# Batch 1's score products in a block-sparse attention and MLP kernel: four 64x64 array tiles, or the whole array with zeros in q

## The chip, the cores and the metric

The kernel runs on one core of one Trainium2 chip. The metric is the device time of one launch in microseconds. The notes below use the engines' short names: TensorE (PE in the profile, PEld its weight loads), VectorE (DVE), ScalarE (ACT), GpSimd (POOL), and SyncE (SP), which issues most of the DMAs.

## The reference

Three stages follow one another. The attention has 2 batches, 8 heads, 768 positions and a head size of 64. Each query sees the keys within 16 positions of its own, and 24 block keys (the maximum over each block of 32 keys), whose values are block means:

```python
k_sum = k.reshape(B, H, nb, block, D).max(axis=3)
v_sum = v.reshape(B, H, nb, block, D).mean(axis=3)
scores_l = scale * np.matmul(q, k.transpose(0, 1, 3, 2))
mask_l = np.abs(pos[:, None] - pos[None, :]) < window
scores_s = scale * np.einsum('bhsd,bhnd->bhsn', q, k_sum) + np.log(block)
...
out = softmax(concat([where(mask_l, scores_l, -1e9), scores_s])) @ concat([v, v_sum])
```

The result, as 2 x 768 rows of 512, goes through a gated two-layer network (token shift with mu, w_k of 512x1024, a squared relu, w_v, and a sigmoid gate by w_r) and then through a mixer (w_tok1, w_tok2 over positions, w_ch1 and w_ch2 over channels, 512x1536 and back). All is f32.

## The kernel before

**Attention.** Work goes by tiles of 128 queries: 6 tiles for each batch. Heads are taken in pairs: the 128 partitions of q and k hold the 64 values of head 2p on rows 0 to 63 and those of head 2p+1 on rows 64 to 127, for four pairs p. A tile of 128 queries needs two key ranges, one for each half of 64 queries: 96 local keys and 24 block keys, 120 columns in all (NC). `kw` holds keys and block keys so that the range of half 0 starts at column 0 and that of half 1 at WC - NC; `k_max` (VectorE) and `kw_sums` (POOL, L293) write the block keys.

`s_stage` (L355 to L391) makes the scores. Before, each product takes the 64 rows of one head and 64 queries and writes 64 partitions of a PSUM bank, so it uses a quarter of TensorE's array; the four combinations of head and half use the four quarters. In batch 0 the stage runs for one head of each pair at a time (`es` has one member), in batch 1 for both heads at once, with 16 matmuls per tile and their order on the queue fixed by `in_line`. There are two score banks (tag "s"), one for each head e. After the products VectorE adds the mask, scales and finds the minimum (L385, four per bank), ScalarE takes the exponential and the row sums (L387), POOL normalizes in batch 1 (`n_stage`, L399), TensorE transposes (`t_stage`, L405), and `v_stage` (L425) multiplies with the values into the bank "pv", which ScalarE copies to `xT`.

**Order.** `attention()` and `main()` are generators. `main()` makes the first network: `ko` matmuls (hidden layer, in groups of 24), `k2_tile` (squared relu) and `values` (`acc` matmuls, in groups of 12). The loop at L674 takes steps of `main()` by a credit after each step of `attention()`, and a weight step (`weights.step`, with ScalarE, VectorE and POOL work) now and then. The final order on each engine is made by a planner that simulates the program with its own costs; `after` and `behind` are ordering hints to it. An engine's queue is in order. SP's queue issues the loads: `q_load` (L353), `k_load`, `vt_load`, `vw_load`. `prep_next` places batch 1's first loads during batch 0; later query tiles are loaded two tiles ahead, into three buffers (QB).

**Masks.** Three masks (inner, first and last tile) are made at L645 to L663 on POOL; rows 0 to 63 hold half 0 and rows 64 to 127 half 1.

Of the kernel before, what the change touches and what calls it, by code (L numbers as in the profile page):

```python
# [9 lines left out]
F32 = mybir.dt.float32  # L10
# [4 lines left out]
ALU = mybir.AluOpType  # L15
# [39 lines left out]


@with_exitstack
def fused_kernel(ctx, tc, q, k, v, vt, mu, w_k, w_v, w_r, w_t1, w_t2, w_c1, w_c2, out):
    nc = tc.nc
    B, NT = q.shape[:2]  # L60
    S, DM = v.shape[1] - WINDOW * 2, v.shape[2]
    H, D = 8, 64
    DFF = w_v.shape[0]
# [158 lines left out]
    def in_line(inst):  # L222

        behind(inst, line[-1:])
        line.append(inst)
# [7 lines left out]
    def after(inst):  # L233

        behind(inst, mark[-1:])
# [31 lines left out]
    def st_of(b):  # L267
        if b not in state:
            state[b] = {"kw": {}, "qT": {}, "vw": {}, "pv": {}, "den": {}}
            state[b]["ks"] = at.tile([128, NP, NB], F32, tag="ks", bufs=2, name="ks")  # L270
        return state[b]
# [17 lines left out]
    @ahead(HK)  # L289
    def kw_sums(b, t):  # L290
        st = state[b]
        for o in (0, WC - NB):
            nc.gpsimd.tensor_scalar(st["kw"][t][:, :, o:o + NB], st["ks"], 1.0, 1.0, ALU.mult, ALU.mult)  # L293
# [53 lines left out]
    @ahead(HL)  # L347
    def q_load(b, t):
        if b == 0:
            st_of(b)["qT"][t] = xT[:, :, XB + 1 + 128 * t:XB + 129 + 128 * t]  # L350
        else:
            st_of(b)["qT"][t] = at.tile([128, NP, 128], F32, tag="qT", bufs=QB, name="qT")
        after(nc.sync.dma_start(st_of(b)["qT"][t], q[b, t]))  # L353

    @ahead(HS)  # L355
    def s_stage(b, t, es):
        st = state[b]
        mask = masks[1 if t == 0 else 2 if t == NT - 1 else 0]
        kw, qT = st["kw"][t], st["qT"][t]
        sps = [bank("s", 2, [128, NP, NC], "sp") for _ in es]  # L360
        line.clear()
        for p in range(NP):
            for half in range(2):
                c0 = half * (WC - NC)
                for sp, e in zip(sps[::-1], es[::-1]):
                    r = slice(64 * e, 64 * e + 64)
                    m = nc.tensor.matmul(sp[64 * half:64 * half + 64, p], qT[r, p, 64 * half:64 * half + 64],  # L367
                                         kw[r, p, c0:c0 + NC], start=True, stop=True)
                    if len(es) > 1:
                        in_line(m)  # L370
        if PINL:
            mark.append(m)
        zs = []
        for sp, e in zip(sps, es):
            mn = at.tile([128, NP], F32, tag="mn", bufs=4, name="mn")
            if b not in LATE:
                den = at.tile([128, NP], F32, tag="den", bufs=4, name="den")
            else:
                if e == 0:
                    st["den"][t] = at.tile([128, 2, NP], F32, tag="dens", bufs=3, name="dens")  # L380
                den = st["den"][t][:, e]
            P = []
            for p in range(NP):
                pe = at.tile([128, NC], F32, tag="pe", bufs=PEB, name="pe")
                low = nc.vector.tensor_tensor_reduce(out=pe, in0=sp[:, p], in1=mask, op0=ALU.add, op1=ALU.min,  # L385
                                                     scale=-1.0 / math.sqrt(D), scalar=3.0e38, accum_out=mn[:, p:p + 1])
                nc.scalar.activation(pe, pe, AF.Exp, bias=mn[:, p:p + 1], scale=-1.0, accum_out=den[:, p:p + 1])  # L387
                P.append(pe)
            lows.append(low)
            zs.append({"u": (b, t, e), "P": P, "den": den})  # L390
        return zs  # L391
# [20 lines left out]
    @ahead(HV)  # L412
    def v_stage(zs):
        b, t, _ = zs[0]["u"]
        st = state[b]
        if t not in st["pv"]:
            st["pv"][t] = bank("pv", 1, [128, NP, 128], "pv")
        pv = st["pv"][t]
        line.clear()
        for p in range(NP):  # L420
            for half in range(2):
                for z in zs[::-1]:
                    e = z["u"][2]
                    h = 2 * p + e
                    m = nc.tensor.matmul(pv[64 * e:64 * e + 64, p, 64 * half:64 * half + 64],  # L425
                                         st["vw"][t][half][0][:, h * D:(h + 1) * D],
                                         z["PT"][:, p, 64 * half:64 * half + 64], start=True, stop=True)
                    if len(zs) > 1:
                        in_line(m)
        if zs[-1]["u"][2] == 1:  # L430
            c0 = b * XB + 1 + 128 * t
            if b not in LATE:
                nc.scalar.copy(xT[:, :, c0:c0 + 128], pv)
            else:
                den = st["den"].pop(t)
                nc.vector.tensor_scalar(den, den, 1e-9, None, ALU.add)
                nc.vector.reciprocal(den, den)
                rb = bank("pt", 2, [128, NP, 128], "rb")
                for p in range(NP):
                    for e in range(2):  # L440
                        nc.tensor.matmul(rb[64 * e:64 * e + 64, p], den[:, e, p:p + 1].to_broadcast([128, D]), ident,
                                         start=True, stop=True)
                x = xT[:, :, c0:c0 + 128]
                nc.scalar.copy(x, pv)
                nc.vector.tensor_tensor(x, x, rb, ALU.mult)
# [64 lines left out]
            q_load(b, 1)  # L510

    def prep(b):

        for t in range(NT):
            k_max(b, t)
            yield HOLD / (NT + 2)
        for j in range(2):
            vt_sum(b, j)
            yield HOLD / (NT + 2)
        kw_sums(b, 0)  # L520
        v_gather(b)
# [120 lines left out]
            q_load(0, t + 1)  # L642
    while weights.todo:
        weights.load()
    masks = []  # L645
    for kind in range(3):
        mc = at.tile([128, NC], F32, name=f"mask{kind}")
        mm = work.tile([128, 2, 128], F32, tag="t32", bufs=2, name="mm")
        for half in range(2):
            m = mm[:, half, :NC]  # L650
            nc.gpsimd.memset(m, 0.0)
            first = 64 * half - PAD
            keys = m[:, NB:NC] if half == 0 else m[:, 0:NK]
            for base, cm, st in ((first + EDGE, -1, 1), (EDGE - first, 1, -1)):
                nc.gpsimd.affine_select(out=keys, in_=keys, pattern=[[st, NK]], compare_op=ALU.is_ge, fill=-8.0 * BIG,
                                        base=base, channel_multiplier=cm)
            if kind == 1 and half == 0:
                nc.gpsimd.memset(m[:, NB:NB + PAD], -8.0 * BIG)
            if kind == 2 and half == 1:
                nc.gpsimd.memset(m[:, NK - PAD:NK], -8.0 * BIG)  # L660
            nc.gpsimd.memset(m[:, 0:NB] if half == 0 else m[:, NK:NC], math.sqrt(D) * math.log(BLOCK))
            nc.gpsimd.tensor_scalar(mc[64 * half:64 * half + 64], m[64 * half:64 * half + 64], 1.0, 1.0, ALU.mult, ALU.mult)
        masks.append(mc)  # L663
    for t in range(NT):
        ahead(HK)(k_max)(0, t)
    kw_sums(0, 0)
    for z in range(B):
        nc.gpsimd.memset(xT[:, :, z * XB:z * XB + 1], 0.0)
    nc.gpsimd.tensor_scalar(oms, mus, -1.0, 1.0, ALU.mult, ALU.add)
# [412 lines left out]
    for got in cd():  # L1082
# [10 lines left out]
    const.release()  # L1093


_INS = ['q', 'k', 'v', 'vt', 'mu', 'moe_w_k', 'moe_w_v', 'moe_w_r',
        'moe2_w_tok1', 'moe2_w_tok2', 'moe2_w_ch1', 'moe2_w_ch2']


def laid_out(q, k, v, mu_k, mu_r, w_k):  # L1100

    import numpy as np

    B, H, S, D = q.shape
    nt = S // 128

    def by_values(x):
        return x.reshape(B, H // 2, 2, x.shape[2], D).transpose(0, 2, 4, 1, 3).reshape(B, 2 * D, H // 2, x.shape[2])

    pad = ((0, 0), (0, 0), (WINDOW, WINDOW), (0, 0))  # L1110
    kp = by_values(np.pad(k, pad))
    dm, dff = w_k.shape
    return {
        "q": by_values(q).reshape(B, 2 * D, H // 2, nt, 128).transpose(0, 3, 1, 2, 4),
        "k": np.stack([kp[..., 128 * t:128 * t + 128 + 2 * WINDOW] for t in range(nt)], axis=1),
        "v": np.pad(v, pad).transpose(0, 2, 1, 3).reshape(B, S + 2 * WINDOW, H * D),
        "vt": by_values(v).reshape(B, 2 * D, 2, H // 4 * S).transpose(0, 2, 1, 3),
        "mu": np.concatenate([m.reshape(-1, 128).T for m in (mu_k, mu_r)], axis=1),
        "moe_w_k": w_k.reshape(dm // 128, 128, dff // 128, 128).transpose(2, 1, 0, 3).reshape(dff // 128, 128, dm),
    }  # L1120
# [22 lines left out]
```

## Time and profile before

| | |
|---|---|
| median of 3 runs | 503.41 us |
| runs | 502.32 to 503.72 us |
| profiled execution, span | 502.8 us |
| profiled execution, own time beside its span | not listed apart from the runs above; the median is 0.6 us over the span |
| mean granted TensorE clock | 0.990 of full speed |
| TensorE, VectorE, ScalarE, POOL busy | 97%, 63%, 50%, 43% |

The span runs from the first to the last instruction of one profiled execution. Matmuls are pipelined and their recorded durations overlap, so what one costs is read from the distance between starts. In the rows, "64*64 64x120" means weights of 64 rows by 64 columns and a moving operand of 64 partitions by 120 columns. A bracket at the end of a row is the idle time ahead of it and what ended it; "issue" means that the profile shows no releaser. f32 matmuls are recorded as two instructions each, transposes as one.

### The profile page before, as it was taken

Reading aid. Unit: us, or ns where it says so; the run is one execution under the profiler, and the core shown is the slowest. Engines: PE = TensorE matmul, PEld = TensorE weight load, DVE = VectorE, ACT = ScalarE, POOL = GpSimd, SP = SyncE. Lnnn points to the kernel's source line nnn. Section 1 sums busy time; section 2 is a strip of 40 time slices with the busy share of each in tenths; the row PEclk is TensorE's granted clock in tenths of the full one; section 3 lists DMA queues with packets and bytes.
Section 4 is the critical chain, followed back from the end, with each engine's and each line's share of the span. In section 5 each row is a group of like instructions: output and inputs, shape, how many; then the busy total and the mean of one; then the engine's idle time right before and its main releaser. Section 6 shows DMA issues by size and latency. Waiting matters only on the chain.

```text
span 502.8 us, 8800 instructions
## 1 busy us (share of the span) xinstructions
PE 487.9 (97%) x3278; PEld 407.1 (81%) x3278; DVE 316.6 (63%) x638; ACT 250.9 (50%) x569; POOL 217.4 (43%) x266
## 2 busy tenths in 40 slices
PE   7999997999999999999999998999999999999996
PEld 3567785888888888888888887878898999989995
DVE  2888998641514355598889789646579638354352
ACT  1778746862544555686585455454554435111110
POOL 6335587862441447345516434774942813000000
PEclk9899998899999999999999999999999999999999
DMA  8999930221000650000551998639351405253102
GB/s 264 323 309 361 335 87 14 88 80 40 20 1 2 224 196 0 1 0 14 161 163 21 400 394 313 211 112 316 117 168 42 142 31 164 52 200 117 52 1 83
DMA packets 35914, 70.63 MB, mean 140 GB/s; under 512 B 3072, under 2 KB 12288, under 8 KB 35872
## 3 DMA queue, kind: packets, MB, share of 16 engines
q1 hardware_dynamic: 34288, 69.09, 42.0%
q10 hardware_dynamic: 1584, 0.98, 0.7%
q8 instruction: 26, 0.43, 0.3%
q14 instruction: 16, 0.13, 0.1%
HBM read 60.04 MB, written 9.44 MB: 138 GB/s over the span
## 4 chain that ended last, share of the span: by engine, by line
PE 75%; DMA 10%; DVE 8%; POOL 2%; ACT 2%; issue 1%; SPq 1%; DVEq 0%; POOLq 0%
PE ko L544 13%; PE acc L544 13%; PE o L955 12%; PE m L544 11%; PE o L983 7%; PE ro L544 7%; PE go L544 5%; DMA wst<-in_moe_w_k_dram 3%; DMA xT<-in_q_dram 3%; DMA ybuf<-in_v_dram 2%; DVE wf L163 2%; PE pv L425 2%; PE sp L367 2%; PE h L544 2%; DMA wst<-in_moe_w_ch_dram 1%
## 5 line engine op out<-in xcount | busy, mean ns | idle before, releaser
L175 POOL TENSOR_TENSOR w<-wf,w 128x512 fp32r<-128x512 f32 x50 | 69.1, 1387 | 77.3 <-ACT w L174 72.4
L544 PE MATMUL ko<-xh,w 128*128 128x256 f32 x384 | 76.3, 288 | 1.7 <-POOL w L175 0.9
L544 PE MATMUL m<-u,w 128*128 128x256 f32 x504 | 65.1, 283 | 0.8 <-DVE mw L846 0.7
L544 PEld LDWEIGHTS m<-u,w 128*128 128x128 f32 x504 | 63.4, 191 | 2.9 <-DVE mw L846 0.9
L544 PEld LDWEIGHTS ko<-xh,w 128*128 128x128 f32 x384 | 61.1, 188 | 5.4 <-POOL w L175 1.1
L544 PE MATMUL acc<-w,kh 128*128 128x512 f32 x192 | 61.7, 404 | 0.0
L955 PE MATMUL o<-w,gh 128*128 128x512 f32 x192 | 59.1, 391 | 0.0
L544 PE MATMUL ko<-xl,w 128*128 128x256 f32 x192 | 54.4, 283 | 1.1 <-DVE xl L536 1.1
L559 POOL TENSOR_TENSOR kl<-rl,kh 128x512 fp32r<-128x512 f32 x24 | 33.7, 1405 | 44.6 <-ACT kh L558 36.4
L163 DVE SCALAR_TENSOR_TENSOR wf<-wst,wf 128x512 int32<-128x512 int32 x50 | 47.6, 956 | 8.2 <-ACT wst L153 7.1
L174 ACT CAST w<-wf 128x512 fp32r<-128x512 f32 x50 | 30.9, 620 | 42.8 <-DVE wf L163 40.9
L557 DVE TENSOR_TENSOR rl<-rl 128x512 f32<-128x512 f32 x24 | 19.6, 819 | 48.4 <-ACT rl L556 48.2
L387 ACT ACTIVATE pe<-pe,mn 128x120 f32<-128x120 f32 x96 | 36.6, 383 | 14.6 <-DVE mn L385 14.3
L153 ACT ACTIVATE wst<-wst 128x512 f32<-128x512 f32 x62 | 41.1, 675 | 2.1 <-DMA wst<-in_moe_w_ch_dram 2.1
L544 PEld LDWEIGHTS acc<-w,kh 128*128 128x128 f32 x192 | 35.3, 192 | 7.3 <-ACT pe L387 0.3
L955 PEld LDWEIGHTS o<-w,gh 128*128 128x128 f32 x192 | 34.7, 188 | 6.2
L534 DVE SCALAR_TENSOR_TENSOR xk<-xT,mus,tmp 128x256 f32<-128x256 f32 x52 | 36.5, 733 | 4.1 <-POOL tmp L533 3.2
L544 PEld LDWEIGHTS ko<-xl,w 128*128 128x128 f32 x192 | 36.2, 188 | 2.1 <-DVE xl L536 1.3
L544 PE MATMUL acc<-w,kl 128*128 128x512 f32 x96 | 37.7, 403 | 0.0
L955 PE MATMUL o<-w,gl 128*128 128x512 f32 x96 | 37.1, 391 | 0.0
L544 PE MATMUL go<-u,w 128*128 128x512 f32 x144 | 35.6, 393 | 0.0
L784 ACT ACTIVATE gh<-m 128x512 fp32r<-128x512 f32 x24 | 14.2, 596 | 42.7 <-DVE m L846 42.7
(120 smaller groups left out, 964.5 us busy)
## 6 DMA issues: line engine op xcount, KB each, us to landing
wst<-in_moe_w_ch_dram SPq DMA_DIRECT2D x36, 512.0 KB, 6.9
w<-stored SPq DMA_DIRECT2D x24, 512.0 KB, 4.9
stored<-w SPq DMA_DIRECT2D x24, 256.0 KB, 4.7
wst<-in_moe_w_k_dram SPq DMA_DIRECT2D x8, 512.0 KB, 7.4
wst<-in_moe_w_v_dram SPq DMA_DIRECT2D x8, 512.0 KB, 9.5
wst<-in_moe_w_tok_dram SPq DMA_DIRECT2D x6, 512.0 KB, 4.7
out_dram<-o SPq DMA_DIRECT2D x12, 256.0 KB, 2.4
kw<-in_k_dram SPq DMA_DIRECT2D x9, 320.0 KB, 5.1
```

The costliest lines, as they stand in the source:

```text
L153: a = nc.scalar.activation(top.bitcast(F32), top.bitcast(F32), AF.Prelu, scale=2.0 ** -112, alpha=2.0 ** 32)
L163: nc.vector.scalar_tensor_tensor(wi, top, 3, wi, ALU.logical_shift_left, ALU.bitwise_or)
L174: r = nc.scalar.copy(hi, src)
L175: eng.tensor_tensor(lo, src, hi.bitcast(F32), ALU.subtract)
L387: nc.scalar.activation(pe, pe, AF.Exp, bias=mn[:, p:p + 1], scale=-1.0, accum_out=den[:, p:p + 1])
L534: nc.vector.scalar_tensor_tensor(xk[:, d], xT[:, d, x0:x0 + MW], mu[:, d:d + 1], tmp, ALU.mult, ALU.add)
L544: nc.tensor.matmul(o, l, r, start=(first and i == 0), stop=(last and i == 3 * n - 1))
L557: nc.vector.tensor_tensor(rl, rl, rl, ALU.mult)
L559: nc.gpsimd.tensor_tensor(lo, rl, hi.bitcast(F32), ALU.subtract)
L784: nc.scalar.activation(hi, o, AF.Relu)
L955: nc.tensor.matmul(accs[c][t], l, r, start=(first and j == 0 and i == 0), stop=(last and j == 1 and i == 2))
L983: nc.tensor.matmul(accs[0][t], l, r, start=(k == 0 and i == 0), stop=(k == NF2 - 1 and i == 2))
```

## The change

In batch 1 the scores become products over the whole array. A new input `qd` holds batch 1's queries as weights of 128 rows by 128 columns for each pair and half: columns 0 to 63 are the half's queries of head 2p, with zeros in the rows of head 2p+1, and columns 64 to 127 the other way round. One product gives both heads' scores of 64 queries, so a tile takes 8 matmuls in place of 16, and a bank holds one half of the queries for both heads, no longer one head for both halves. The masks follow (`both`, eight copies on POOL), and so do the reads of the transposed probabilities in `v_stage`. The query tile of batch 1 doubles in size, and less of the on-chip memory is set aside by `dynamic_dma_scratch_size`. Batch 0 keeps its products.

```diff
     def q_load(b, t):
         if b == 0:
             st_of(b)["qT"][t] = xT[:, :, XB + 1 + 128 * t:XB + 129 + 128 * t]
+            after(nc.sync.dma_start(st_of(b)["qT"][t], q[t]))
         else:
-            st_of(b)["qT"][t] = at.tile([128, NP, 128], F32, tag="qT", bufs=QB, name="qT")
-        after(nc.sync.dma_start(st_of(b)["qT"][t], q[b, t]))
+            st_of(b)["qT"][t] = at.tile([128, NP, 2, 128], F32, tag="qT", bufs=QB, name="qT")
+            after(nc.sync.dma_start(st_of(b)["qT"][t], qd[b - 1, t]))
 
     def s_stage(b, t, es):
         st = state[b]
-        mask = masks[1 if t == 0 else 2 if t == NT - 1 else 0]
         kw, qT = st["kw"][t], st["qT"][t]
         sps = [bank("s", 2, [128, NP, NC], "sp") for _ in es]
-        line.clear()
-        for p in range(NP):
-            for half in range(2):
+        if len(es) == 1:
+            mask = [masks[1 if t == 0 else 2 if t == NT - 1 else 0]]
+            r = slice(64 * es[0], 64 * es[0] + 64)
+            for p in range(NP):
+                for half in range(2):
+                    c0 = half * (WC - NC)
+                    m = nc.tensor.matmul(sps[0][64 * half:64 * half + 64, p], qT[r, p, 64 * half:64 * half + 64],
+                                         kw[r, p, c0:c0 + NC], start=True, stop=True)
+        else:
+            mask = [both[:, 1 if t == 0 else 0], both[:, 3 if t == NT - 1 else 2]]
+            line.clear()
+            for half, sp in enumerate(sps):
                 c0 = half * (WC - NC)
-                for sp, e in zip(sps[::-1], es[::-1]):
-                    r = slice(64 * e, 64 * e + 64)
-                    m = nc.tensor.matmul(sp[64 * half:64 * half + 64, p], qT[r, p, 64 * half:64 * half + 64],
-                                         kw[r, p, c0:c0 + NC], start=True, stop=True)
-                    if len(es) > 1:
-                        in_line(m)
+                for p in range(NP):
+                    m = nc.tensor.matmul(sp[:, p], qT[:, p, half], kw[:, p, c0:c0 + NC], start=True, stop=True)
+                    in_line(m)
...
-        for sp, e in zip(sps, es):
+        for sp, e, mk in zip(sps, es, mask):
...
-                low = nc.vector.tensor_tensor_reduce(out=pe, in0=sp[:, p], in1=mask, op0=ALU.add, op1=ALU.min,
+                low = nc.vector.tensor_tensor_reduce(out=pe, in0=sp[:, p], in1=mk, op0=ALU.add, op1=ALU.min,
...
     def v_stage(zs):
-                for z in zs[::-1]:
-                    e = z["u"][2]
+                for e in (1, 0) if len(zs) > 1 else (zs[0]["u"][2],):
                     h = 2 * p + e
+                    z, c = (zs[half], e) if len(zs) > 1 else (zs[0], half)
                     m = nc.tensor.matmul(pv[64 * e:64 * e + 64, p, 64 * half:64 * half + 64],
                                          st["vw"][t][half][0][:, h * D:(h + 1) * D],
-                                         z["PT"][:, p, 64 * half:64 * half + 64], start=True, stop=True)
+                                         z["PT"][:, p, 64 * c:64 * c + 64], start=True, stop=True)
...
+    both = at.tile([128, 4, NC], F32, name="both")
+    for i, (kind, half) in enumerate(((0, 0), (1, 0), (0, 1), (2, 1))):
+        for e in range(2):
+            rows.append((both[64 * e:64 * e + 64, i], masks[kind][64 * half:64 * half + 64]))
     for t in range(NT):
         ahead(HK)(k_max)(0, t)
     kw_sums(0, 0)
+    for dst, src in rows:
+        nc.gpsimd.tensor_copy(dst, src)
...
+    qt = by_values(q).reshape(B, 2 * D, H // 2, nt, 128).transpose(0, 3, 1, 2, 4)
+    qd = np.zeros((B - 1, nt, 2, D, H // 2, 2, 2, 64), q.dtype)
+    for e in range(2):
+        qd[:, :, e, :, :, :, e] = qt[1:, :, e * D:e * D + D].reshape(B - 1, nt, D, H // 2, 2, 64)
...
-    nc = bacc.Bacc("TRN2", target_bir_lowering=False, num_devices=1)
+    nc = bacc.Bacc("TRN2", target_bir_lowering=False, num_devices=1, dynamic_dma_scratch_size=1024)
```

## Rows read from the trace of the kernel before

**Rows 1.** The page: engines' busy time, and the chain's shares by engine.

```profile
PE 487.9 (97%) x3278; PEld 407.1 (81%) x3278; DVE 316.6 (63%) x638; ACT 250.9 (50%) x569; POOL 217.4 (43%) x266
...
PE 75%; DMA 10%; DVE 8%; POOL 2%; ACT 2%; issue 1%; SPq 1%; DVEq 0%; POOLq 0%
```

**Rows 2.** Groups by line: batch 1's scores; busy us, mean ns, idle before.

```profile
L367 PE MATMUL sp<-kw,qT 64*64 64x120 f32 x192 | 11.7, 299 | 1.6 <-issue 1.5
```

**Rows 3.** The chain in order of time: start us, us, what.

```profile
112.34 0.44 PE pt L405 x4
...
151.72 2.84 PE ko L544 x24
154.56 2.80 PE acc L544 x12
157.35 0.56 PE sp L367 x14
157.92 3.03 PE ko L544 x24
...
163.75 0.36 PE sp L367 x6
```

**Rows 4.** TensorE's timeline: start us, us covered, line, operation, count, idle before.

```profile
17.48 1.02 PE L623 MATMUL spin<-ident 128*128 128x512 f32 x2
18.34 0.38 PE L405 MATMUL pt<-ident,pe 128*120 128x128 f32 x2
...
71.06 1.04 PE L367 MATMUL sp<-kw,qT 64*64 64x120 f32 x28
...
84.71 0.63 PE L367 MATMUL sp<-kw,qT 64*64 64x120 f32 x2 [1.52 <-issue]
...
163.68 0.43 PE L367 MATMUL sp<-kw,qT 64*64 64x120 f32 x6
```

**Rows 5.** Windows of 2 us: PE, PEld, DVE, ACT, POOL, clock, DMA, GB/s.

```profile
80.00:82.00 2.00, 0.75 (x4) 0.55 (x5) 2.00 (x2) 0.27 (x1) 2.00 (x3) 1.00 0.00 0
82.00:84.00 2.00, 1.20 (x10) 0.99 (x9) 2.00 (x7) 1.72 (x4) 1.63 (x2) 0.98 0.00 0
84.00:86.00 2.00, 1.29 (x4) 0.91 (x5) 2.00 (x16) 2.00 (x10) 2.00 (x3) 0.50 0.10 25
...
90.00:92.00 2.00, 2.00 (x9) 1.59 (x9) 1.54 (x13) 2.00 (x12) 2.00 (x4) 0.81 0.89 273
```

**Rows 6.** VectorE's timeline: the first and the fourth read of a bank.

```profile
83.73 0.27 DVE L385 CUSTOM_DVE_ANT_0 pe<-sp,mask 128x120 f32<-128x120 f32 x1
...
84.33 0.27 DVE L385 CUSTOM_DVE_ANT_0 pe<-sp,mask 128x120 f32<-128x120 f32 x1
```

**Rows 7.** SP's timeline: batch 1's first and third query load, last keys.

```profile
49.52 0.72 SPq L353 DMA_DIRECT2D qT<-in_q_dram  x1
...
52.97 1.21 SPq L280 DMA_DIRECT2D kw<-in_k_dram  x2
...
60.69 0.35 SPq L353 DMA_DIRECT2D qT<-in_q_dram  x1
```

**Rows 8.** Windows of 2 us, columns as in rows 5.

```profile
54.00:56.00 2.00, 2.00 (x17) 2.00 (x18) 2.00 (x5) 1.20 (x4) 0.99 (x2) 1.00 1.12 384
...
64.00:66.00 2.00, 2.00 (x20) 2.00 (x19) 2.00 (x3) 2.00 (x4) 0.40 (x1) 1.00 1.02 226
66.00:68.00 2.00, 2.00 (x15) 1.66 (x14) 2.00 (x4) 1.09 (x3) 2.00 (x2) 1.00 0.38 120
```

**Rows 9.** VectorE's timeline: the last key reductions and the second value sum.

```profile
67.10 1.27 DVE L287 TENSOR_REDUCE ks<-kw 128x16 f32<-128x512 f32 x2
...
71.69 1.74 DVE L309 TENSOR_REDUCE vrs<-ybuf 128x48 f32<-128x1536 f32 x1
```

**Rows 10.** POOL's timeline: the last mask write and the first block sums.

```profile
7.05 0.29 POOL L662 TENSOR_SCALAR mask<-mm 64x120 f32<-64x120 f32 x1
11.34 2.85 POOL L293 TENSOR_SCALAR kw<-ks 128x96 f32<-128x96 f32 x12 [4.00 <-DVE ks L287]
```

More of the change, by code (lines that the diff above doesn't have):

```diff
@@ L57, in fused_kernel @@
 @with_exitstack
-def fused_kernel(ctx, tc, q, k, v, vt, mu, w_k, w_v, w_r, w_t1, w_t2, w_c1, w_c2, out):
+def fused_kernel(ctx, tc, q, qd, k, v, vt, mu, w_k, w_v, w_r, w_t1, w_t2, w_c1, w_c2, out):
     nc = tc.nc
-    B, NT = q.shape[:2]
+    B, NT = k.shape[:2]
     S, DM = v.shape[1] - WINDOW * 2, v.shape[2]
@@ L644, in fused_kernel @@
         weights.load()
-    masks = []
+    masks, rows = [], []
     for kind in range(3):
@@ L1093, in fused_kernel @@
     const.release()
-_INS = ['q', 'k', 'v', 'vt', 'mu', 'moe_w_k', 'moe_w_v', 'moe_w_r',
+_INS = ['q', 'qd', 'k', 'v', 'vt', 'mu', 'moe_w_k', 'moe_w_v', 'moe_w_r',
         'moe2_w_tok1', 'moe2_w_tok2', 'moe2_w_ch1', 'moe2_w_ch2']
@@ L1112, in laid_out @@
     dm, dff = w_k.shape
+    qt = by_values(q).reshape(B, 2 * D, H // 2, nt, 128).transpose(0, 3, 1, 2, 4)
+    qd = np.zeros((B - 1, nt, 2, D, H // 2, 2, 2, 64), q.dtype)
+    for e in range(2):
+        qd[:, :, e, :, :, :, e] = qt[1:, :, e * D:e * D + D].reshape(B - 1, nt, D, H // 2, 2, 64)
     return {
-        "q": by_values(q).reshape(B, 2 * D, H // 2, nt, 128).transpose(0, 3, 1, 2, 4),
+        "q": qt[0], "qd": qd.reshape(B - 1, nt, 2 * D, H // 2, 2, 128),
         "k": np.stack([kp[..., 128 * t:128 * t + 128 + 2 * WINDOW] for t in range(nt)], axis=1),
```

## The prediction

> **What bounds the kernel now.** I read the page first. TensorE is busy 97% of the span, and the chain that ended last is TensorE for three quarters of it [rows 1]: what shortens TensorE's own queue shortens the kernel, unless the time comes back as a wait. The changed products are one line, 192 instructions that cover 11.7 us (96 matmuls, each recorded as two) [rows 2]. That mean hides their cost, so I went to the chain in order of time and the TensorE timeline, where they stand between their neighbours.
>
> From about 98 us on the chain is nearly all TensorE, and there the price of a score group can be read cleanly [rows 3]. A run of 24 ko matmuls takes 2.84 us when it follows acc matmuls, but 3.03 us when it follows score products: about 0.20 us is paid on leaving them. The 14 products take 0.56 us and the 6 take 0.36 us, so one more product costs 0.20/8 = 0.025 us, and a group costs 0.36 + 0.20 - 6 x 0.025 = 0.41 us beyond its products. Four transposes, f32 on the whole array, take 0.44 us between acc runs, which is 0.11 us each with nothing left over. So the 64x64 products stream fast, four abreast, but every entry and exit costs.
>
> The six tiles of batch 1 are cut by the planner into 18 such groups, the first and last of which stand in [rows 4]; by tile they are 3, 2, 2, 3, 4 and 4. One tile falls into a bad place: TensorE idles in 80 to 84 us, waits 1.52 us for the second tile's first product, and its clock is at 0.50, the 1.2 GHz level, from 84 to a little past 90 us [rows 4, 5]. That wait ends when VectorE finishes its fourth read of the previous scores, near 84.5 us, which frees the bank [rows 6].
>
> **The change, part by part.**
>
> *The products.* Removed: 192 instructions and 18 entries and exits. At full clock that is 18 x 0.41 + 192 x 0.025 = 7.4 + 4.8 = 12.2 us. Added: 96 instructions on the whole array, 120 columns each. No row shows exactly this form. Nearest below: the spin products, f32 on the whole array, take 0.86 us for two (17.48 to 18.34) with 512 columns, 0.43 us each, and 120/512 of that is 0.101 us [rows 4]; 96 are 9.7 us. Nearest above, with a full-width weight load for every instruction: the ko run, 2.84/24 = 0.118 us [rows 3]; 96 are 11.3 us. The transposes' 0.110 us for 128 columns lies between and is the nearest kin; 120 columns of it would be 0.103 us, and if the weight load sets the pace it stays at 0.110. I take 0.106 us, 10.2 us in all. Gain at full clock 12.2 - 10.2 = 2.0 us, with ends 0.9 and 2.5 us. One tile runs at the lower clock, where streaming doubles: there whole-array products stream 16 x 0.106 = 1.7 us more, the tiled ones 32 x 0.025 = 0.8 us more, and part of the entry costs doubles too. I take 0.3 us off for that: a gain of 1.7 us.
>
> The row on leaving a group shows 0.20 us of delay and no such delay for transposes [rows 3]. The Trainium skill's page "TensorEngine Tiling (Array Packing)", section Key Properties, says that changing the tiling mode drains the engine; the trace agrees, with 0.41 us per group. The same page speaks against this change in its section When to Use Tiling: for a contraction of 64 it wants row tiles. By that alone the sum would lose the abreast streaming, 10.2 against 4.8 us, and come out 5.4 us worse; the entries and exits decide, and that is a rival below.
>
> *Order.* The products now go by half, so one bank is complete after 8 instructions instead of 32. VectorE may start its four reads about 0.8 us earlier (8 x 0.106), which is cover, not path: in the bad place VectorE comes to these reads late for reasons of its own queue, not for the products. Zero, and that is where an upside may sit. The value products now take the first half from one score tile and the second from the other; the first needs half the keys of both heads from one tile only, but they stay in one line and end with the same last operand. Zero. Reads, exponentials, normalization and transposes keep their number and shapes.
>
> *Loads.* A batch-1 query tile is 512 KB instead of 256 KB, six of them, with its zeros. Three are issued at 49.5 to 61 us [rows 7], into a full queue: DMA's share is above 1.0 through 66 us and 0.38 in the 2 us after [rows 8]. At 54 to 56 us it moves 384 GB/s, so 256 KB more is 0.7 us; three put off what follows by up to 2.1 us. Behind the first of them on SP's queue stand key tiles and the second half of the value sums. The last key reductions start at 67.10 us and the second value sum at 71.69 us, both after VectorE was continuously busy [rows 9], while the queue emptied near 66.5 us; the value sum has 5 us of cover, and the last keys, issued at 52.97 us [rows 7], have one extra load ahead of them, 0.7 us against 14 us until they are read. Zero, with an upper end of 0.7 us. The other three are issued from 89 us with a nearly free queue. Zero.
>
> *Masks.* Eight copies of 64x120 on POOL near the start. The nearest row, a mask write of that size, is 0.29 us, so 2.3 us. POOL idles 4.00 us ahead of the block sums of 11.34 us [rows 10], and the masks are done at 7.3 us. Zero; without that cover 2.3 us would stand before the first scores, which wait for the block sums.
>
> *Sum.* 503.41 - 1.7 = 501.7 us. The profiled execution has a span of 502.8 us, and 0.6 us around it gives the median shown (runs 502.32 to 503.72), so the sum needs no correction.
>
> **The rivals.**
>
> *The stall goes too.* The planner sets its order afresh. If VectorE's reads of the first tile come earlier, the 1.52 us wait at 83.19 us vanishes, and with it perhaps the low clock, which costs half of some 7 us, 3.5 us: 501.7 - 5.0 = 496.7 us, or about 499 with half of it. For it: the bank is complete sooner. Against: VectorE is busy without a break from 80 to 84 us [rows 5], and its order is not the products' doing.
>
> *Another such stall* (slower). The second four products of a tile need the second bank, all four of them, and TensorE's queue behind them holds the ko and acc matmuls. Where VectorE's reads of the last tile are placed late, TensorE idles, and the clock falls again as at 84 us. Price 1.5 + 3.5 us: 501.7 + 5.0 = 506.7 us. It decides once a stall is added to idle time already there, as in 80 to 84 us; a lone wait of 1.5 us would leave 503.2 us. Against it: over the whole span VectorE is busy 63% [rows 1], so such crowding is rare.
>
> *The packing was worth more* (slower). If the new products still drain, because they border on other column-tiled products, 18 x 0.41 + 10.2 = 17.6 against 12.2 us: 503.41 + 5.4 = 508.8 us. This is the page's rule as a mechanism; the transposes without overhead speak against it.
>
> *The time is freed and not used*: the shorter score groups are filled by waits for weights or for relu, and the kernel stays at 503 us.
>
> **How the numbers follow.** About 0.3%, 1.5 us, is what a measurement of this kernel can tell from no change: under 501.9 is faster, over 504.9 slower. Forecast: 0.50, with its own range 501.0 to 502.6, so 0.28 faster and 0.22 same. Stall gone: 0.22, faster. Another stall: 0.17, slower. Packing: 0.04, slower. Not used: 0.07, same. Together 0.50 faster, 0.29 same, 0.21 slower. The range reaches into the stall cases on both sides and leaves out their far ends and the packing case: 498.0 to 506.0.
>
> **What would show it.** The score line with 96 instructions, each 128 wide and about 0.106 us apart; the ko run after scores at 2.84 us; a group's fixed cost gone. The 80 to 92 us windows tell the two stall cases apart by idle time and clock. I am wrong if the products come over 0.125 us apart (12.2/96, no gain left), if fixed costs remain, or if the time moves by over 3 us in waits between 50 and 100 us.

## The result, and the profile after

The changed kernel takes 509.03 us (508.5 to 509.68), against 503.41 us shown before. Measured side by side, where the kernel before had a median of 504.54 us over nine runs, the ratio is 1.0096, with a 95% interval of 1.0072 to 1.012. It is slower by about 1%. The forecast was 501.7 us, in a range of 498.0 to 506.0 us. Some runs show a lower clock and a time over 1.5% longer whatever the kernel; they are left out of all ratios and of the times of the experiments below.

The page of the changed kernel, engines and chain, answers to [rows 1]:

```profile
PE 492.6 (97%) x3182; PEld 412.8 (81%) x3182; DVE 316.0 (62%) x638; ACT 250.6 (49%) x569; POOL 218.1 (43%) x274
...
PE 76%; DMA 11%; DVE 8%; ACT 2%; POOL 1%; issue 1%; SPq 0%; DVEq 0%
```

TensorE has 96 instructions fewer and is busy 4.7 us longer (492.6 against 487.9); the span grew by 4.4 us. So the time did not go into waits: it lies on TensorE's own queue. Which instructions took it shows in the groups by line. First batch 1's scores and value products in the changed kernel (busy us, mean ns, idle before):

```profile
L376 PE MATMUL sp<-kw,qT 128*128 128x120 f32 x96 | 13.4, 279 | 1.8 <-DVE mn L392 1.4 <-POOL kw L293 0.4
L432 PE MATMUL pv<-PT,vw 120*64 120x64 f32 x192 | 13.1, 233 | 0.0
```

and the value products, the same 192 instructions, in the kernel before:

```profile
L425 PE MATMUL pv<-PT,vw 120*64 120x64 f32 x192 | 7.5, 226 | 0.0
```

They cover 13.1 us instead of 7.5, though nothing in their number or shape was changed. The chain of the changed kernel in order of time shows how (start us, us, what):

```profile
99.75 0.86 PE sp L376 x6
100.61 0.96 PE pv L432 x28
101.58 3.03 PE ko L550 x24
104.61 0.87 PE pt L412 x8
105.48 0.89 PE sp L376 x8
106.37 0.94 PE acc L550 x4
...
123.53 0.42 PE acc L550
123.95 0.26 PE pv L432 x2
124.21 0.42 PE acc L550
124.64 0.26 PE pv L432 x2
124.90 0.42 PE acc L550
125.32 0.26 PE pv L432 x2
```

The upper part is as forecast: eight whole-array score products take 0.89 us, 0.111 us each, and the four acc matmuls behind them their plain 0.94 us. The lower part is new. From 122.4 to 131.6 us one tile's value products stand one matmul at a time (two recorded instructions) between single acc and ko matmuls. A pair of them and the acc matmul behind it take 0.26 + 0.42 = 0.68 us; the acc matmul alone is 2.80/12 = 0.23 us [rows 3] and the pair inside a long run 0.96/28 x 2 = 0.07 us. Each such group therefore costs 0.38 us beyond its work. The value products write 64 of 128 columns of the array, as the old score products did, and pay about the same fee for entering and leaving. On TensorE's timeline the value products of batch 1 form 8 groups in the kernel before and 30 in the changed one: 22 x 0.38 = 8.4 us more.

All the loss lies between TensorE's first and last acc matmul. That stretch, from the starts on its timeline, is 190.3 us before and 196.2 us after; what comes ahead of it is 1.2 us shorter, what follows 0.2 us shorter (246.4 and 246.1). The 1.2 us are no gain of the change: in the profiled execution of the kernel before the clock was lower near 14 us (0.56 and 0.58 in the two windows of 12 to 16 us), and in that of the changed kernel it was full there.

The bad place of [rows 5] is idle as before but keeps its clock. Windows of the changed kernel, with the columns of [rows 5]:

```profile
80.00:82.00 2.00, 0.85 (x9) 0.67 (x7) 2.00 (x12) 2.00 (x6) 1.64 (x3) 1.00 0.22 53
82.00:84.00 2.00, 1.11 (x8) 0.93 (x8) 2.00 (x7) 2.00 (x9) 1.46 (x3) 1.00 0.29 68
84.00:86.00 2.00, 1.74 (x13) 1.55 (x14) 2.00 (x12) 2.00 (x11) 2.00 (x4) 1.00 0.73 248
```

### The profile page after: what moved, and what is told of

Same layout as the page of the kernel before. It is cut to its first block, busy times and chain, and to the rows that moved or that the text cites. A ratio compares the mean times of both kernels' runs of the same rounds, so it can differ in the third digit from the quotient of the medians.

```text
span 507.2 us, 8634 instructions
## 1 busy us (share of the span) xinstructions
PE 492.6 (97%) x3182; PEld 412.8 (81%) x3182; DVE 316.0 (62%) x638; ACT 250.6 (49%) x569; POOL 218.1 (43%) x274
## 4 chain that ended last, share of the span: by engine, by line
PE 76%; DMA 11%; DVE 8%; ACT 2%; POOL 1%; issue 1%; SPq 0%; DVEq 0%
PE acc L550 13%; PE o L967 12%; PE ko L550 12%; PE m L550 11%; PE ro L550 7%; PE o L995 6%; PE go L550 5%; DMA ybuf<-in_v_dram 4%; PE h L550 3%; DMA kw<-in_k_dram 3%; PE pv L432 2%; DMA wst<-in_moe_w_k_dram 2%; PE ho L550 2%; DVE wf L163 2%; DMA qT<-in_qd_dram 1%; DVE wf L157 1%
## 5 line engine op out<-in xcount | busy, mean ns | idle before, releaser
L163 DVE SCALAR_TENSOR_TENSOR wf<-wst,wf 128x512 int32<-128x512 int32 x50 | 49.6, 997 | 4.5 <-ACT wst L153 3.5
## 6 DMA issues: line engine op xcount, KB each, us to landing
wst<-in_moe_w_v_dram SPq DMA_DIRECT2D x8, 512.0 KB, 10.2
```

Source lines behind the costliest of these rows:

```text
L163: nc.vector.scalar_tensor_tensor(wi, top, 3, wi, ALU.logical_shift_left, ALU.bitwise_or)
```

## The experiments

Theory A: the planner, whose order had shifted, cut the value products into more groups, and each costs about 0.39 us. Rival B: the doubled loads or mask copies delay batch 1. Rival C: the whole-array products themselves cost more than four abreast, which is the forecast's packing rival. The table gathers the runs; groups are runs of consecutive products on TensorE's timeline, and "stretch" is the distance between the starts of the first and the last acc matmul. Groups and stretch are those of the one profiled execution; the time is the median of the runs. The ratio of each run is to the kernel before, measured beside it.

| kernel | value groups | score groups | stretch us | time us |
|---|---|---|---|---|
| before | 8 | 18 tiled | 190.3 | 503.4 |
| changed | 30 | 13 whole | 196.2 | 509.0 |
| e1 changed, values first | 12 | 13 whole | 189.2 | 502.7 |
| e2 before, values late | 25 | 16 tiled | 195.0 | 508.6 |
| e3 loads alone | 18 | 26 tiled | 198.3 | 511.9 |
| e4 before, values first | 6 | 18 tiled | 189.7 | 502.6 |
| e5 before, scores whole, both batches | 6 | 10 tiled | 189.0 | 504.2 |
| e6 changed, values in one group | 6 | 13 whole | 187.2 | 499.8 |
| e7 loads alone, values first | 6 | 25 tiled | 193.0 | 508.1 |
| e8 as e1, score products doubled | 12 | 21 whole | 197.3 | 511.5 |
| e9 before, scores whole in batch 1 | 6 | 10 tiled | 185.5 | 499.7 |
| e10 as e6, single loads | 6 | 13 whole | 187.3 | 500.5 |
| e11 products alone | 33 | 13 whole | 197.6 | 510.7 |

**e1, the changed kernel with its value products ahead.** `ahead(n)` gives the planner's order a lead of n places. Only batch 1's lead is changed:

```diff
-    @ahead(HV)
     def v_stage(zs):
+        ahead(HV if len(zs) == 1 else 500)(v_products)(zs)
+
+    def v_products(zs):
```

> The changed kernel with batch 1's value products 500 places ahead in the planner's order instead of 400. On TensorE's queue these 96 products then stand in 12 groups, no longer in 30; the score products keep 13 groups. Theory A (cut value products: every group of column-tiled products between whole-array ones costs about 0.39 us): 18 groups fewer, 18 x 0.39 = 7.0 us less, about 502 us. Rival B (the doubled query loads and the mask copies delay batch 1): the loads stay, so about 509 us. Rival C (the whole-array score products themselves cost more than four abreast): they stay, so about 509 us.

502.69 us, ratio 0.9979 (0.996 to 0.9999). With every load, copy and whole-array product of the change in place, its loss is gone: B and C fall as causes of it. The stretch shrank by 196.2 - 189.2 = 7.0 us for 18 groups, 0.39 us each. The chain of this kernel, from where the changed one alternated:

```profile
118.11 2.37 PE ko L552 x20
120.48 0.96 PE pv L434 x28
121.45 0.68 PE ko L552 x4
122.12 2.81 PE acc L552 x12
```

Two products of each tile (four recorded instructions) still go ahead of the other 28 instructions, hence 12 groups.

**e2, the kernel before with its value products late.** The same edit in the old kernel, with 300.

```diff
+        ahead(HV if len(zs) == 1 else 300)(v_products)(zs)
```

> The kernel before with batch 1's value products 300 places ahead instead of 400: 25 groups of value products instead of 8, 16 of score products instead of 18, nothing else. Theory A: 15 groups more at 0.39 us, 5.9 us more, about 509 us, the same as the changed kernel without any whole-array product. Rivals B and C: no load and no product is changed, so about 503.5 us.

508.62 us, the middle one of three runs from 507.59 to 512.43, ratio 1.0113 (1.0055 to 1.017). A loss like that of the change arises in a kernel that has none of its parts: the stretch is 4.7 us longer, for 15 value groups more and 2 score groups fewer. The profiled execution is the run of 512.43 us and has 2.7 us more ahead of the stretch; there the clock was at 0.50 from 12 to 20 us, so these 2.7 us are not counted. Its chain has the same pattern and the same 0.26 and 0.43 us:

```profile
114.80 0.26 PE pv L427 x2
115.06 0.43 PE acc L546
115.48 0.26 PE pv L427 x2
115.74 0.43 PE acc L546
```

**e3, the loads alone.** The changed kernel's layout of q, loads and mask copies, but the old products, which read their 64 columns from the larger tile (`qT[r, p, half, r]`), and the old value products.

> The changed kernel with its doubled query loads and mask copies, but with the old tiled score products and the old value products. The planner cuts it into 18 groups of value and 26 of score products (8 and 18 before). Theory A: 18 groups more at 0.39 us, 7 us more, about 510.5 us. Rival B: the loads alone give the whole loss, about 509 us. Rival C: about 503.5 us. A and B are close here; the trace tells them apart by where TensorE loses the time, between products or waiting ahead of batch 1's first scores.

511.86 us, ratio 1.0171 (1.0126 to 1.0215). Its value products alternate too, and its first acc matmul starts at 64.5 us, as in e4 (64.6 us), which has the old loads: nothing is lost ahead of the stretch, where late loads would hold up batch 1's first scores. This shows that the cutting needs no whole-array product: the planner takes another order when the loads alone are changed. What the loads cost beyond that is not told by this run.

**e4, the kernel before with whole value products.** As e2, with 600.

> The kernel before with batch 1's value products 600 places ahead: 6 groups of value products instead of 8, one for each tile, and 18 of score products as before. Theory A: 2 groups fewer, 0.8 us less, about 502.7 us. Rivals B and C: no difference, 503.5 us. This is also the base against which the change is compared fairly, with value products whole in both.

502.63 us, ratio 0.9976 (0.9937 to 1.0015): inside the noise, and as forecast by A, so the time alone decides nothing here. The stretch shrank by 0.6 us for 2 groups.

**e5, tiled scores in whole groups.** As e4, with `HS` from 0 to 300, which is the lead of the score stage.

> The kernel before with batch 1's value products 600 places ahead and its attention's score stage 300 places ahead: the old tiled score products in 10 groups instead of 18, the value products in 6. Theory A (each group of tiled products between whole-array ones costs about 0.4 us, whichever product it is): 8 x 0.41 less than the kernel with whole value products (502.7), 499.4 us, faster than the changed kernel in any form so far, with no zeros and no new layout. Rival C' (the number of groups matters for the value products only, since score groups only fill idle time): 502.7 us as with the value products alone.

504.17 us, ratio 1.0015 (0.9976 to 1.0053): a miss against 499.4. The 32 tiled instructions of a tile did run together in four of the six tiles, but two things went against it. `HS` moved batch 0's scores as well, and in the profiled execution TensorE reached its first acc matmul at 70.4 us instead of 64.6 in e4. It was busy for only 3.27 of the 5 us from 30 us on, and the clock fell. The page's clock row of this run shows it in the third and fourth slice (25 to 50 us), where e4's has 9:

```profile
PEclk9977998989999999999999999999999999999999
```

And the stretch itself is only 0.7 us shorter than in e4, where A gave 3.3: TensorE waits 5.4 us in it instead of 3.3. So the run tested two things; e9 tests the one.

**e6, the value products in one group.** As e1, and the halves are taken in the other order, so that the first product needs the operand that is ready last.

```diff
-            for half in range(2):
+            for half in (1, 0) if len(zs) > 1 else (0, 1):
                 for e in (1, 0) if len(zs) > 1 else (zs[0]["u"][2],):
```

> The changed kernel with value products 500 places ahead, and the halves taken in the other order, so that the first product needs the operand that is ready last and all 16 follow at once: 6 groups instead of 12, score groups as before. Theory A: 6 x 0.39 = 2.3 us less than with 12 groups (502.7), 500.4 us. Rival (the order of the two score tiles in the value products doesn't matter): 502.7 us.

499.84 us, ratio 0.9927 (0.99 to 0.9955), faster than both kernels. Against e1 the stretch is 2.0 us shorter for 6 groups. The kernel before had this order by its reversed loop over the heads' tiles; with one score tile for each half the change lost it. The chain of e6, one tile:

```profile
116.23 0.66 PE sp L376 x6
116.89 0.13 PE ko L552
117.02 1.08 PE pv L434 x32
118.10 2.92 PE ko L552 x23
```

**e7, the loads alone, values first.** As e3, with the lead of 500.

> Doubled loads and mask copies with the old tiled products, value products 500 places ahead: 6 groups of value and 25 of score products. Theory A: 5 groups more than the kernel before (31 against 26), 2 us more, 505.4 us. Rival B (the loads cost by themselves): the loss of the loads-alone run stays, about 511 us.

508.05 us, ratio 1.009 (1.0059 to 1.0122), 2.7 us over what A gave. The stretch is 3.4 us longer than in e4 for 7 groups more, 2.7 us by A. Another 3.1 us arises before it: the first acc matmul starts at 67.7 us instead of 64.6 in e4. In the profiled execution the clock is low near the start; this row is of e7, 10 to 20 us:

```profile
10.00:20.00 10.00, 8.57 (x57) 4.83 (x57) 6.85 (x29) 4.49 (x22) 4.03 (x17) 0.67 1.08 327
```

and the same 10 us of e1, where the clock is full:

```profile
10.00:20.00 10.00, 9.06 (x88) 5.14 (x88) 7.63 (x38) 6.20 (x31) 4.21 (x18) 1.00 1.07 340
```

Batch 1's loads are issued 30 us later and can't be the reason, and such a low stretch also stands in the kernel before (12 to 16 us) and in e2 (12 to 20 us), which have neither doubled loads nor mask copies. So the 3.1 us are not shown to be a cost of the loads. Why the clock falls there stays open.

**e8, each whole-array product twice.**

```diff
                     m = nc.tensor.matmul(sp[:, p], qT[:, p, half], kw[:, p, c0:c0 + NC], start=True, stop=True)
                     in_line(m)
+                    m = nc.tensor.matmul(sp[:, p], qT[:, p, half], kw[:, p, c0:c0 + NC], start=True, stop=True)
+                    in_line(m)
```

> The changed kernel with value products 500 places ahead, each whole-array score product issued twice. 96 recorded instructions more, value products still in 12 groups. If a product costs 0.1125 us on the path wherever it stands and no entry or exit: 96 x 0.1125 = 10.8 us more, 513.5 us. If it partly fills idle time of TensorE: less, 505 to 510 us. If entries count for them as well (21 groups instead of 13, at 0.4): 3 us on top, 516.5 us.

511.49 us, ratio 1.0173 (1.0121 to 1.0225), 8.8 us over e1 and not 10.8: a part filled idle time (TensorE's waits in the stretch fell from 3.7 to 1.5 us). The products lie on the path at nearly their full price, and 8 more groups of them show no sign of a fee.

**e9, tiled scores whole, in batch 1 alone.** As e4, and the score stage gets a lead of 500 where both heads are taken (`len(es) > 1`).

> The kernel before with value products 600 places ahead and, in batch 1 alone, the score stage 500 places ahead; batch 0 keeps its order, which the earlier run with whole tiled scores did not. Score products in 10 groups instead of 18, value products in 6. Theory A: 8 x 0.41 = 3.3 us less than with whole value products alone (502.7), 499.4 us, level with the best whole-array kernel (499.8). Rival (score groups fill idle time, or scores pulled forward leave TensorE waiting on VectorE later): 502.7 us or more, with the idle time in the trace.

499.68 us, ratio 0.9917 (0.9885 to 0.995): as forecast by A, level with e6. The stretch is 4.2 us shorter than in e4, for 8 score groups fewer. The old tiled products, unchanged, give the same time once their groups are few. TensorE's timeline shows a tile's 32 instructions in 1.05 us where they run whole, in three of the six tiles (the others are split in 2, 2 and 3):

```profile
70.79 1.05 PE L369 MATMUL sp<-kw,qT 64*64 64x120 f32 x32
...
94.75 1.05 PE L369 MATMUL sp<-kw,qT 64*64 64x120 f32 x32
98.16 1.05 PE L369 MATMUL sp<-kw,qT 64*64 64x120 f32 x32
```

**e10, single loads.** As e6, but three query tiles are cleared once and two loads of 128 KB write the diagonal blocks.

```diff
-            st_of(b)["qT"][t] = at.tile([128, NP, 2, 128], F32, tag="qT", bufs=QB, name="qT")
-            after(nc.sync.dma_start(st_of(b)["qT"][t], qd[b - 1, t]))
+            z = st_of(b)["qT"][t] = zq[t % QB]
+            for e in range(2):
+                r = slice(64 * e, 64 * e + 64)
+                after(nc.sync.dma_start(z[r, :, :, r], qs[b - 1, t, r]))
...
+        nc.gpsimd.memset(zq[i], 0.0)
```

> The best whole-array kernel so far (value products 500 places ahead, halves in the other order, 6 groups) with single-size query loads: three query tiles are cleared once, and two 128 KB loads write their diagonal blocks, so that no zeros are loaded. The planner's groups are the same. If the doubled loads cost nothing by themselves: 499.8 us as there. Rival B (they put off batch 1's first tiles): 0.7 to 2.1 us less, 497.7 to 499.1 us.

500.52 us, ratio 0.9927 (0.9902 to 0.9952), the same ratio as e6; the stretch is the same too (187.3 and 187.2 us). The zeros in the loads cost nothing that can be measured.

**e11, the products alone.** As e10, with the change's own lead and order of halves.

> The changed kernel with single-size query loads as in the run beside it, with the change's own lead of 400 places and its own order of halves: whole-array products without the doubled loads. The planner cuts the value products into 33 groups. Theory A: as the changed kernel with 3 groups more, 509.0 + 1.2 = 510.2 us. Rival B (the doubled loads bring the loss): 502 to 503.5 us.

510.73 us, ratio 1.0146 (1.0099 to 1.0193). Without the doubled loads the loss is there, and larger with 33 groups.

## Why the prediction was wrong

**The score products: right.** They were forecast at 0.106 us each, 10.2 us in all, with no entry fee. In the changed kernel the time from each to the next start, less TensorE's waits, adds up to 10.95 us, 0.114 each or 0.7 us more than forecast, and acc matmuls run at their plain pace behind them. The fee of 0.41 us for a tiled group was near as well: 0.39 us by e1, 0.34 by e6, 0.32 by e4 and 0.36 by e2 (13 groups more in all), and 0.52 by e9 against e4. With the value products alike in both (e6 against e4, 6 groups each), the stretch is 2.5 us shorter with whole-array products, where the forecast gave 1.7. The low clock at 84 us, which e4 has and e6 has not, may have a share in that. It need not be large: e10 has the same products in the same order as e6, its clock was at 0.50 in 86 to 88 us, and its stretch is the same.

**The step that failed** is "The value products now take the first half from one score tile and the second from the other ... Zero", together with the count "18 entries and exits". The fee was read from the score products and applied to them alone, though the value products are column-tiled and pay it too. I took their grouping, 8 groups, as given. It was not: it hung on the planner, and the change moved it to 30. 22 x 0.38 = 8.4 us more, less the 2.5 us that e6 against e4 gives for the rest of the change, is the 5.9 us by which the stretch grew.

Two things made the groups. The order of halves splits off the first two products of every tile, because their operand is ready before the rest (e6 against e1: 2.0 us). The larger part is the planner's lead: 400 places were just enough before and are too few after. The orders that the planner makes with other leads, which were not run, show the margin: in the kernel before 360 places give 15 groups, 380 give 7 and 420 give 6; in the changed kernel 440 places give 16, 460 give 13 and 470 give 12. That the lead runs out because more of the first network's matmuls stand ahead in program order, not yet issued, is an argument and wasn't tested. That loads alone (e3) and products alone (e11) both trigger it is shown: it is the margin that was thin, not one part of the change that is bad.

**The rivals.** "The packing was worth more" named this mechanism, products that "border on other column-tiled products", gave it 0.04 and the time 508.8 us. The time came near by luck, since the place was wrong: the whole-array products pay nothing and the value products do. The page "TensorEngine Tiling (Array Packing)" of the Trainium skill has both halves of the matter: the drain at a change of mode, section Key Properties, with which the trace agrees at 0.3 to 0.5 us for a group, and row tiling for a contraction of 64, section When to Use Tiling. On that one e9 shows a draw here: tiled products in 10 groups do as well as whole-array products with zeros, and no better. That the fee comes from the change of mode, and not from the narrow shape of the products, is not separated by any run; the products inside a long group cost no fee (0.96 us for 28).

"The stall goes too" was half right: the clock stayed full, the idle time remained. Its price of 3.5 us for the low clock is not borne out by e10 against e6. "Another such stall" didn't happen; TensorE's waits in the stretch are 3.7 us against 3.2.

**Costed at zero, and zero:** the loads (e10), and the mask copies, for which POOL still has idle time left ahead of the block sums in the changed kernel:

```profile
11.10 2.85 POOL L293 TENSOR_SCALAR kw<-ks 128x96 f32<-128x96 f32 x12 [2.53 <-DVE ks L287]
```

4.00 us were idle there before [rows 10].

## What to carry to other kernels

Where a fee hangs on entering and leaving a kind of work, list every instruction that pays it, not only those that the change removes, and count the groups in the planned order of each: a kernel whose order a planner makes can lose on untouched instructions. After such a change look first at groups by line whose count is the same and whose busy time grew. And before a layout is rebuilt to avoid a fee, try the cheap cure: longer leads for two stages in batch 1 (e9) gave the old products 3.7 us without a zero being loaded.

## What the runs showed that I had not expected

The clock at 84 us does not follow from the order of the work or from the idle time. TensorE idles three times in the kernel before around the fall: for 0.74, 0.93 and 1.52 us, the last of them the wait of [rows 4].

```profile
80.32 0.39 PE L544 MATMUL ko<-xh,w 128*128 128x256 f32 x1 [0.74 <-ACT rl L556]
81.75 0.50 PE L544 MATMUL ko<-xh,w 128*128 128x256 f32 x2 [0.93 <-POOL w L175]
```

In e2 the same instructions stand there with the same idle pieces:

```profile
83.06 0.38 PE L546 MATMUL ko<-xh,w 128*128 128x256 f32 x1 [0.76 <-ACT rl L558]
84.49 0.50 PE L546 MATMUL ko<-xh,w 128*128 128x256 f32 x2 [0.93 <-POOL w L175]
...
87.45 0.39 PE L367 MATMUL sp<-kw,qT 64*64 64x120 f32 x2 [1.52 <-issue]
```

In the kernel before the granted clock is at 0.50, the 1.2 GHz level, from 84 us on [rows 5]. In e2 it stays at the 2.4 GHz level through the stall and behind it:

```profile
86.00:88.00 2.00, 0.55 (x3) 0.42 (x4) 2.00 (x17) 2.00 (x8) 2.00 (x2) 1.00 0.00 0
88.00:90.00 2.00, 2.00 (x35) 1.41 (x35) 2.00 (x5) 2.00 (x11) 1.30 (x2) 1.00 0.30 70
```

e6 and e10 are a second such pair: one order on TensorE, idle pieces of 1.20, 0.90 and 0.25 us in e6 and of 1.13, 0.90 and 0.25 us in e10, and the clock falls in e10 alone, with no change in the stretch. So that the changed kernel kept its clock in its profiled execution can't be put down to the change. What decides it no run here shows.
